# Two attention-and-spectral layers on one core: a second pair of row-sum accumulators, the row-sum matmul moved behind a product with V, the last group's output sums and the weights' maxima redistributed

## The chip, the cores and the metric

The kernel runs on 1 core of one Trainium2 chip. The metric is device time in microseconds (us) of one execution; a kernel's time is the median of its runs. TensorE (PE in the profile; its weight loads are PEld) does the matrix products, VectorE (DVE) elementwise work and reductions, ScalarE (ACT) the exponentials, copies and casts, GpSimd (POOL) small elementwise work, and SyncE (SP) issues nearly all transfers. Matmul results lie in PSUM, everything else on the chip in SBUF.

## The reference

x is 2048 rows of 1024. Two layers follow each other, with the same weights, and each is an attention block and a spectral block:

```python
def _A_ref(x, wqkv, wo):
    qkv = (x @ wqkv).reshape(B, S, 3, H, Dh).transpose(2, 0, 3, 1, 4)     # H = 32, Dh = 32
    q, k, v = qkv[0], qkv[1], qkv[2]
    scores = einsum("bhqd,bhkd->bhqk", q, k) * (Dh ** -0.5)
    o = einsum("bhqk,bhkd->bhqd", softmax(scores), v)
    return o.transpose(0, 2, 1, 3).reshape(B, S, D) @ wo

def _B_ref(x, w_r, w_i):
    X = rfft2(x, axes=(-2, -1)) * (w_r + 1j * w_i)
    return irfft2(X, s=(S, D), axes=(-2, -1))

for _ in range(2):
    x = x + _A_ref(_layernorm(x), A_wqkv, A_wo)
    x = x + _B_ref(_layernorm(x), B_w_r, B_w_i)
```

All values are float32. The kernel splits many operands into a high and a low float16 part and adds three products. That needs the inputs to lie in a range, so while it runs it gathers maxima of the weights and of a few statistics ("flags"); at the end `combine_flags` makes one number of them, by which a general version of the whole would run instead. With these inputs it does not run.

## The kernel before

**Layers.** `build` calls `attention` (L270) and `spectral` (L750) for layer 0 and layer 1. Layer 0 alone gathers the weights' maxima.

**Attention: start.** Rows are normalised, split and transposed by transfers, and the first values, keys and queries are made.

**Attention: the loop (L625 to L676).** The 32 heads are 8 groups `g` of 4. For each group there are 4 chunks `c` of 512 queries, and for each chunk 16 tiles `kt` of 128 keys. One step (g, c, kt) is:

- `S`: 12 matmuls (L558), 32 rows of the array each, give the scores of 4 heads in two PSUM tiles of 128x1024. The pool `psS` has 3 such tiles. ScalarE makes two exponentials `p` of 128x1024 from them (L562); the pool for `p` has 8 tiles, so four steps.
- `PV`: 4 products of `p` with V (L568), each in 32 columns of the array, added up over kt in PSUM (`psO`, one tile). They run two steps at a time, at even kt, for the two steps before.
- `add`: VectorE adds the two halves of `p` to the accumulators `acc` (L581; at kt = 1 it starts them from two tiles, L579).

When the last key tile of a chunk has been added, `fin` follows, at kt = 1 of the next chunk, after that step's scores: 4 matmuls with a matrix of ones (L587) turn `acc` into row sums in a third `psS` tile, VectorE transposes it, takes reciprocals, transposes back and scales the output (L588 to L594). At kt = 5 `out` splits the output into two float16 parts (L600, L601) and stores it, or keeps it in SBUF in the last group.

Two steps make a slot, kt even and kt odd. At the end of each slot TensorE gets other work as a fill, from generators that yield after each matmul or two: keys, queries and values of the next groups (L340, L384), and, in the last two groups, the product with the output weights. There a row tile t (128 rows, of chunk t // 4) is done in two parts. `wo_part` does the first 7 of 8 head groups: per half of 512 columns 21 matmuls (L443) and one VectorE eviction onto the residual (L466). `wo_rest` does the eighth group when its output is there: 6 matmuls into a `psS` tile, one 128x1024 eviction (L475), two statistics (L477), a store (L478), their aggregation (L498). Tiles 0 to 11 are done so inside the loop, tiles 2 and 3 partly in group 6. In group 7 a slot has either 21 matmuls of a part or one `wo_rest`; the first eleven slots have parts, and later the two alternate.

**Attention: the tail (L677 to L733).** The last chunk's row sums and output, then row tiles 12 to 15 (`first`, `last`, `whole`), and the other tiles are normalised and folded into the layout of the spectral block (L513, L146, L147).

**Spectral.** A first stage of 32 steps transposes (L791), multiplies (L800) and splits with ScalarE and VectorE (L804, L805). Beside it `absmax` loads the output weights in 16 pieces through 3 buffers and takes their maxima (L784, L785). Then a loop over 32 units (`fb`, `fc`, `binv`, `cinv`): products with constants (L862), copies (L855), products (L894), four VectorE products with the spectral weights (L901 to L904), GpSimd sums, a cast and its low half (L909, L910), and products back (L862, L931). `loadw` loads the weights two units ahead (L834) and takes their maxima (L837, L838). A last stage goes back to rows (L965, L977).

**Order.** TensorE's and ScalarE's order in the attention loop is the program's. Elsewhere, and on VectorE, GpSimd and SP everywhere, a planner fixes the order when the kernel is built, by its own estimate of when each instruction's inputs are there; at run time each engine takes its instructions strictly in that order. So an instruction of the spectral block can stand on VectorE inside the attention's tail.

Of the kernel before, what the change touches and what calls it, by code (L numbers as in the profile page):

```python
# [6 lines left out]
F32 = mybir.dt.float32  # L7
# [181 lines left out]
class AttnPools:  # L189


    def __init__(self, tc):
# [12 lines left out]
        self.acc = [a[:, i] for i in (14, 15)]  # L205
# [21 lines left out]
class Weights:  # L227
# [5 lines left out]
    def prep(self, ph):  # L233
# [36 lines left out]
def attention(nc, tc, layer, ap, xin, yd, wts, wo, cst, dram, flags):  # L270
# [184 lines left out]
    def wo_part(c, t, dst):  # L455

        x = xres(c, t)
        for n in range(2):
            p = bank()
            m = wo_mm(p, c, t, n, range(7))  # L460
            for _ in range(20):
# [4 lines left out]
            nc.vector.scalar_tensor_tensor(dst[:, sl], p, 1.0 / (SO * SW), x[:, sl], op0=ALU.mult, op1=ALU.add)  # L466
            yield
# [15 lines left out]
    def wo_parts():  # L483
        load_o(0)
        load_o(1)
        for t in [2, 3, 0, 1] + list(range(4, 12)):
# [7 lines left out]
    mvs = sm.tile([128, 24], F32, name="mvs")  # L494
# [55 lines left out]
    P, O, acc = {}, {}, ap.acc  # L550
# [24 lines left out]
    def add(g, c, kt):  # L575
        for hf in range(2):
            p = P[g, c, kt, hf]
            if kt == 1:
                nc.vector.scalar_tensor_tensor(acc[hf], P[g, c, 0, hf], 1e-34, p, op0=ALU.add, op1=ALU.add)  # L579
            elif kt:  # L580
                nc.vector.tensor_add(acc[hf], acc[hf], p)  # L581

    def fin(g, c):
        zt = on.tile([128, 16, 32], F32, name="zt")
        z = psS.tile([128, 2, 512], F32, name="s")[:, 0]
        for h in range(4):
            nc.tensor.matmul(z[32 * h:32 * h + 32], cst["ones"], acc[h // 2][:, h % 2], start=True, stop=True)  # L587
# [19 lines left out]
    pend, done, late = [], [], []  # L607
    fill, lwo, wof = filler(), load_wo(), wo_parts()
    left, parts, rests = 16, 20, list(range(12))
# [15 lines left out]
    with tc.manual_schedule(engines={mybir.EngineType.PE, mybir.EngineType.Activation}):  # L625
        for g in range(NG):
# [610 lines left out]
```

## Time and profile before

| | |
|---|---|
| median of 3 runs | 3885.8 us (3885.0 to 3886.59) |
| the profiled execution's own time | 3887.92 us |
| its span, first to last instruction | 3886.0 us |
| mean granted clock of TensorE | 0.988 |
| exponentials (L562) | 2048 x 1112 ns |
| additions to the accumulators (L581) | 1792 x 1218 ns |
| matmuls of a row sum (L587) | 512 records x 593 ns (median), 8 per row sum |
| running maxima, removed by the change: L261, L785, L838 | 48, 16 and 32 on VectorE |

How to read it: in an answer in order of time, each row has the start, the length, the engine, the line and operation, what is written and read, the count of instructions merged into the row, and in brackets the idle time of the engine just before, with what ended it. Lengths of instructions that follow each other overlap a little, so the time that one really takes is the distance between starts. In a view of one line the three figures are the shortest, the median and the longest in ns.

### The profile page before, as it was taken

Reading aid. Unit: us, or ns where it says so; the run is one execution under the profiler, and the core shown is the slowest. Engines: PE = TensorE matmul, PEld = TensorE weight load, DVE = VectorE, ACT = ScalarE, POOL = GpSimd, SP = SyncE. Lnnn points to the kernel's source line nnn. Section 1 sums busy time; section 2 is a strip of 40 time slices with the busy share of each in tenths; the row PEclk is TensorE's granted clock in tenths of the full one; section 3 lists DMA queues with packets and bytes.
Section 4 is the critical chain, followed back from the end, with each engine's and each line's share of the span. In section 5 each row is a group of like instructions: output and inputs, shape, how many; then the busy total and the mean of one; then the engine's idle time right before and its main releaser. Section 6 shows DMA issues by size and latency. Waiting matters only on the chain.

```text
span 3886.0 us, 79635 instructions
## 1 busy us (share of the span) xinstructions
PE 3738.1 (96%) x32951; PEld 1644.2 (42%) x32951; DVE 3181.9 (82%) x3967; ACT 2901.1 (75%) x3567; POOL 304.1 (8%) x386
## 2 busy tenths in 40 slices
PE   6999999999999999989989999999999999999998
PEld 4322433343234233368854334333433432333788
DVE  6689899989998987966675998989899889788544
ACT  4578887888788865657855888888888888666686
POOL 1000000000000000014320000000000000000143
PEclk9999999999999999999999999999999999999999
DMA  8000000000000221134270000000000002111333
GB/s 204 15 12 23 12 12 17 18 12 18 12 26 7 73 70 64 62 142 140 62 179 12 15 23 12 12 18 18 12 20 12 23 12 90 53 69 66 147 99 105
DMA packets 165575, 194.08 MB, mean 50 GB/s; under 512 B 74961, under 2 KB 120657, under 8 KB 164177
## 3 DMA queue, kind: packets, MB, share of 16 engines
q1 hardware_dynamic: 164912, 188.82, 15.6%
q8 instruction: 260, 4.26, 0.5%
q14 instruction: 115, 0.93, 0.1%
q10 hardware_dynamic: 288, 0.07, 0.0%
HBM read 123.83 MB, written 48.23 MB: 44 GB/s over the span
## 4 chain that ended last, share of the span: by engine, by line
PE 73%; DVE 12%; issue 7%; ACT 3%; DMA 3%; POOL 1%; SPq 0%; DVEq 0%; ACTq 0%; POOLq 0%
PE o L568 20%; PE s L558 17%; PE x L340 12%; PE x L384 7%; PE x L443 6%; DVE R L581 3%; ACT p L562 2%; PE ps L862 2%; PE ps L800 2%; PE s L587 1%; PE ps L791 1%; DMA w<-in_w 1%; PE s L443 1%; PE o L384 1%; PE ps L977 1%
## 5 line engine op out<-in xcount | busy, mean ns | idle before, releaser
L562 ACT ACTIVATE p<-s,bias 128x1024 f32<-128x1024 f32 x2048 | 2169.7, 1112 | 575.4 <-PE s L558 564.5
L581 DVE TENSOR_TENSOR R<-R,p 128x1024 f32<-128x1024 f32 x1792 | 2089.0, 1218 | 139.4 <-ACT p L562 136.3
L568 PE MATMUL o<-p,R 128*32 128x512 f32 x8192 | 985.5, 599 | 0.0
L340 PE MATMUL x<-big,wqk 128*128 128x512 f16 x2880 | 684.2, 383 | 17.0 <-DVE Q L168 6.3
L558 PEld LDWEIGHTS <-R 32*128 32x128 f16 x12288 | 233.0, 92 | 769.3 <-issue 654.3
L340 PEld LDWEIGHTS <-wqk 128*128 128x128 f16 x3072 | 277.3, 98 | 452.9 <-issue 159.1
L558 PE MATMUL s<-Q,R 32*128 32x512 f16 x6144 | 433.0, 378 | 12.0 <-ACT p L562 10.7
L558 PE MATMUL s<-R 32*128 32x512 f16 x6144 | 432.3, 379 | 8.2 <-ACT p L562 6.7
L568 PEld LDWEIGHTS o<-p,R 128*32 128x32 f32 x8192 | 213.8, 109 | 524.6 <-issue 524.0
L384 PEld LDWEIGHTS <-big 128*128 128x128 f16 x3072 | 296.5, 100 | 155.5 <-issue 73.9
L384 PE MATMUL x<-wv,big 128*128 128x256 f16 x2688 | 324.1, 277 | 34.5 <-DMA big<-hl 34.5
L579 DVE SCALAR_TENSOR_TENSOR R<-p 128x1024 f32<-128x1024 f32 x128 | 153.9, 1203 | 196.1 <-ACT p L562 195.7
L443 PE MATMUL x<-big 128*128 128x512 f16 x1050 | 237.4, 380 | 0.0
L365 POOL PARTITION_ALL_REDUCE mall<-mqk x16 | 40.7, 2542 | 2333.8 <-DVE mqk L359 2322.5
L443 PEld LDWEIGHTS <-big 128*128 128x128 f16 x1344 | 126.2, 98 | 178.0 <-issue 34.6
L910 DVE TENSOR_TENSOR H<-G,H 128x512 f16<-128x512 f32 (+1 forms) x68 | 46.5, 683 | 105.4 <-ACT H L909 105.3
L862 PE MATMUL ps<-cbi,H 128*128 128x256 f16 (+1 forms) x792 | 99.2, 273 | 6.0 <-ACT H L909 3.7
L855 ACT COPY U<-ps 64x256 f32<-64x256 f32 (+1 forms) x272 | 97.2, 357 | 8.4 <-PE ps L862 3.3
L855 ACT COPY B<-ps 64x256 f32<-64x256 f32 (+1 forms) x272 | 97.1, 357 | 6.7 <-PE ps L862 2.4
L862 PE MATMUL ps<-cb,big 128*128 128x256 f16 x780 | 96.3, 273 | 0.0
L805 DVE TENSOR_TENSOR big<-ps,big 128x512 f16<-128x512 f32 x64 | 44.5, 695 | 58.5 <-ACT big L804 58.5
L167 ACT ACTIVATE R<-x 128x512 f16<-128x512 f32 x88 | 52.7, 598 | 50.5 <-PE x L340 50.4
(429 smaller groups left out, 2992.5 us busy)
## 6 DMA issues: line engine op xcount, KB each, us to landing
wst<-in_wp SPq DMA_DIRECT2D x96, 256.0 KB, 3.0
R<-y SPq DMA_DIRECT2D x32, 512.0 KB, 5.4
w<-in_w SPq DMA_DIRECT2D x60, 256.0 KB, 2.7
od<-ohl SPq DMA_DIRECT2D x56, 256.0 KB, 2.4
big<-od SPq DMA_DIRECT2D x16, 896.0 KB, 6.7
y<-R SPq DMA_DIRECT2D x20, 512.0 KB, 2.7
R<-in_x SPq DMA_DIRECT2D x16, 512.0 KB, 5.8
wst<-in_wo SPq DMA_DIRECT2D x32, 256.0 KB, 3.0
```

The lines of the kernel that those rows point to most:

```text
L167: nc.scalar.activation(hi, src, AF.Copy, scale=scale)
L340: nc.tensor.matmul(ps, a, b, start=d == 0 and i == 0, stop=d == 7 and i == 2)
L384: nc.tensor.matmul(ps[:, j], l, r, start=d == 0 and i == 0, stop=d == 7 and i == 2)
L443: nc.tensor.matmul(p, a, b, start=start and d == ds[0] and i == 0, stop=stop and d == ds[-1] and i == 2)
L558: nc.tensor.matmul(s[h // 2][:, h % 2], K[g][r, a, kt * 128:kt * 128 + 128], Q[g][r, b, c * 512:c * 512 + 512], start=i == 0, stop=i == 2)
L562: nc.scalar.activation(p, s[hf], AF.Exp, bias=bias[g], scale=SCALE / (SQ * SQ))
L568: nc.tensor.matmul(O[g, c][32 * h:32 * h + 32], V[g][:, kt, 32 * h:32 * h + 32], P[g, c, kt, h // 2][:, h % 2], start=kt == 0, stop=kt == ...
L579: nc.vector.scalar_tensor_tensor(acc[hf], P[g, c, 0, hf], 1e-34, p, op0=ALU.add, op1=ALU.add)
L581: nc.vector.tensor_add(acc[hf], acc[hf], p)
L800: nc.tensor.matmul(pa[:, j], tt[:, j], mm[:, g], start=True, stop=True)
L855: nc.scalar.copy(ov[64 * r:64 * r + 64, a0:a0 + m, x], tl[64 * x:64 * x + 64, :m, r])
L862: nc.tensor.matmul(out, l, r, start=k == 0, stop=k == len(mm_) - 1)
```

## The change

1. **Accumulators.** There are now two pairs, `acc0` where the pair was and `acc1` in a new pool of its own; chunk c uses pair c % 2. The reserve for transfer descriptors in SBUF is given as 4096 bytes, and the new pair lies in the space.
2. **Row sums.** `add` of the last key tile now only notes the chunk in `full`; `fin` runs at kt = 2 of the next chunk, right behind that step's two products with V. The fin of the last chunk stays in the tail.
3. **The last group.** `share` gives for each of the 32 slots how many matmuls of `wo_part` it does (21 in ten slots, 7 in six, 11 and 10 in twelve, 12 in four), and `rests` in which slots a `wo_rest` follows them. Tile 11 is done in the last four slots with all 8 head groups at once, with its statistics and store, and has no `wo_rest`.
4. **Maxima.** Each reduction of a piece of the weights writes a column of its own in a table; the running maxima (L261, L785, L838) go, and `combine_flags` reduces the two tables at the end. The reductions of the output weights are held in program order: each stands on VectorE behind the instruction that the program has before it, which is a subtraction of the first spectral stage (L805).

```diff
-        self.acc = [a[:, i] for i in (14, 15)]
+        self.acc0 = [a[:, i] for i in (14, 15)]
...
+        self.accp = small("at_acc", 1)
...
-                wm = ap.sm.tile([128, 1], F32, name="wm")
-                nc.vector.tensor_reduce(wm, st[i], axis=AX.XY, op=ALU.max, apply_absolute_value=True)
-                nc.vector.tensor_max(self.flag, self.flag, wm)
+                nc.vector.tensor_reduce(self.flag.pop(), st[i], axis=AX.XY, op=ALU.max, apply_absolute_value=True)
...
-    def wo_part(c, t, dst):
+    def wo_part(c, t, dst, nd):
 
         x = xres(c, t)
+        st = sm.tile([128, 2, 6], F32, name="st")
         for n in range(2):
             p = bank()
-            m = wo_mm(p, c, t, n, range(7))
-            for _ in range(20):
+            m = wo_mm(p, c, t, n, range(nd))
+            for _ in range(3 * nd - 1):
                 next(m)
                 yield
             run(m)
             sl = slice(n * 512, n * 512 + 512)
             nc.vector.scalar_tensor_tensor(dst[:, sl], p, 1.0 / (SO * SW), x[:, sl], op0=ALU.mult, op1=ALU.add)
+            if nd == 8:
+                nc.vector.bn_stats(st[:, n], dst[:, sl])
+                if n:
+                    r0 = c * 512 + t * 128
+                    nc.sync.dma_start(yd[r0:r0 + 128, :], dst)
+                    nc.vector.bn_aggr(mvs[:, 8 * c + 2 * t:8 * c + 2 * t + 2], st)
             yield
...
-            yield from wo_part(t // 4, t % 4, wo_dst[t])
+            yield from wo_part(t // 4, t % 4, wo_dst[t], 8 if t == 11 else 7)
...
-    P, O, acc = {}, {}, ap.acc
+    P, O = {}, {}
+    acc1 = ap.accp.tile([128, 2, 2, 512], F32, name="acc")
+    acc = [ap.acc0, [acc1[:, i] for i in range(2)]]
...
-            nc.tensor.matmul(z[32 * h:32 * h + 32], cst["ones"], acc[h // 2][:, h % 2], start=True, stop=True)
+            nc.tensor.matmul(z[32 * h:32 * h + 32], cst["ones"], acc[c % 2][h // 2][:, h % 2], start=True, stop=True)
...
-    left, parts, rests = 16, 20, list(range(12))
+    left, rests = 16, {}
+    share = [21] * 10 + [7] * 6 + [11, 10] * 6 + [12] * 4
+    for t, n in zip(range(11), (11, 12, 14, 15, 20, 22, 24, 26, 28, 29, 30)):
+        rests[n] = t
...
                     late = pend
                     pend = []
+                    if kt == 2 and full:
+                        done = [full.pop()]
+                        fin(*done[0])
                 for w in late[:1]:
                     add(*w)
                     if w[2] == NKT - 1:
-                        fin(*w[:2])
-                        done = [w[:2]]
+                        full = [w[:2]]
...
                 elif g == NG - 1:
-                    t = rests[0] if rests else 16
-                    if (t // 4 < c - 1 or t // 4 == c - 1 and kt >= 7) and (kt % 4 == 3 or not parts):
-                        wo_rest(rests.pop(0))
-                    elif parts:
-                        parts -= 1
-                        for _ in range(21):
-                            next(wof)
+                    for _ in range(share[u // 2]):
+                        next(wof)
+                    if u // 2 in rests:
+                        wo_rest(rests[u // 2])
...
-            m = p3.tile([128, 1], F32, name="wom")
-            nc.vector.tensor_reduce(m, wos.pop(0), axis=AX.X, op=ALU.max, apply_absolute_value=True)
-            nc.vector.tensor_max(flags["w"], flags["w"], m)
+            tc.keep_in_program_order(nc.vector.tensor_reduce(flags["wcol"].pop(), wos.pop(0), axis=AX.X, op=ALU.max, apply_absolute_value=True))
...
-            m = p2.tile([128, 1], F32, name="wbm")
-            nc.vector.tensor_reduce(m, wt, axis=AX.X, op=ALU.max, apply_absolute_value=True)
-            nc.vector.tensor_max(flags["wb"], flags["wb"], m)
+            nc.vector.tensor_reduce(flags["wb"][:, i:i + 1], wt, axis=AX.X, op=ALU.max, apply_absolute_value=True)
...
+    fw, fb = (pool.tile([128, 1], F32, name=n) for n in ("fwm", "fwbm"))
+    nc.vector.reduce_max(fw, flags["w"], axis=AX.X)
+    nc.vector.reduce_max(fb, flags["wb"], axis=AX.X)
...
-    nc = _bacc.Bacc("TRN2", target_bir_lowering=False, num_devices=1)
+    nc = _bacc.Bacc("TRN2", target_bir_lowering=False, num_devices=1, dynamic_dma_scratch_size=4096)
```

More of the change, by code (lines that the diff above doesn't have):

```diff
@@ L453, in xres @@
         return x
-    def wo_part(c, t, dst):
+    mvs = sm.tile([128, 24], F32, name="mvs")
+    def wo_part(c, t, dst, nd):
         x = xres(c, t)
+        st = sm.tile([128, 2, 6], F32, name="st")
         for n in range(2):
             p = bank()
-            m = wo_mm(p, c, t, n, range(7))
-            for _ in range(20):
+            m = wo_mm(p, c, t, n, range(nd))
+            for _ in range(3 * nd - 1):
                 next(m)
@@ L485, in wo_parts @@
         load_o(1)
-        for t in [2, 3, 0, 1] + list(range(4, 12)):
+        for t in (2, 3, 0, 1, 4, 5, 6, 7, 8, 9, 10, 11):
             if t == 8:
@@ L605, in out @@
             olast[c] = t
-    pend, done, late = [], [], []
+    pend, done, late, full = [], [], [], []
     fill, lwo, wof = filler(), load_wo(), wo_parts()
-    left, parts, rests = 16, 20, list(range(12))
+    left, rests = 16, {}
+    share = [21] * 10 + [7] * 6 + [11, 10] * 6 + [12] * 4
+    for t, n in zip(range(11), (11, 12, 14, 15, 20, 22, 24, 26, 28, 29, 30)):
+        rests[n] = t
     def slots(f, sums, n, steps):
@@ L674, in attention @@
         run(wof)
-        for t in rests:
-            wo_rest(t)
     with tc.manual_schedule(engines={mybir.EngineType.PE}):
@@ L1173, in build @@
             "mv": cp.tile([128, 32, 2], F32, name="fmv"),
-            "w": cp.tile([128, 1], F32, name="fw"),
-            "wb": cp.tile([128, 1], F32, name="fwb"),
+            "w": cp.tile([128, 64], F32, name="fw"),
+            "wb": cp.tile([128, 32], F32, name="fwb"),
             "r": cp.tile([128, 16], F32, name="fr"),
@@ L1178, in build @@
         }
-        nc.vector.memset(flags["w"], 0.0)
-        nc.vector.memset(flags["wb"], 0.0)
+        flags["wcol"] = [flags["w"][:, i:i + 1] for i in range(64)]
         nc.vector.memset(flags["r"], 0.0)
@@ L1187, in build @@
             nc.sync.dma_start(ap.x[:, t], x[t * 128:(t + 1) * 128, :])
-        wts = [Weights(nc, ap, a["wp"], None if layer else flags["w"]) for layer in range(2)]
+        wts = [Weights(nc, ap, a["wp"], None if layer else flags["wcol"]) for layer in range(2)]
         for layer in range(2):
```

15 lines of the change are left out of this document (8 added, 7 removed).

## The prediction

> **What bounds the kernel now.** I read the page first, then the windows by stage, then the instructions in order of time.
>
> ```profile
> span 3886.0 us, 79635 instructions
> PE 3738.1 (96%) x32951; PEld 1644.2 (42%) x32951; DVE 3181.9 (82%) x3967; ACT 2901.1 (75%) x3567; POOL 304.1 (8%) x386
> PE 73%; DVE 12%; issue 7%; ACT 3%; DMA 3%; POOL 1%; SPq 0%; DVEq 0%; ACTq 0%; POOLq 0%
> ```
>
> TensorE is the bound of the whole, but 4% of the span is not its own. The windows (columns: stretch, its length, busy time of PE, PEld, DVE, ACT and POOL, granted clock, DMA) show where: the last head group of layer 0, then the attention's tail up to the first transpose of the spectral part in layer 0 and layer 1, then the spectral unit loop in layer 0 and layer 1.
>
> ```profile
> 1410.00:1640.00 230.00, 225.15 (x1798) 74.66 (x1787) 186.02 (x203) 138.80 (x136) 0.00 (x0) 1.00 0.17 62
> ...
> 1647.25:1705.26 58.01, 42.88 (x205) 18.76 (x201) 49.28 (x105) 20.14 (x21) 11.62 (x33) 0.90 0.48 161
> 3573.45:3621.30 47.85, 42.72 (x205) 18.77 (x201) 39.43 (x74) 20.03 (x21) 11.64 (x33) 0.98 0.27 95
> ...
> 1755.11:1918.43 163.32, 153.10 (x1303) 135.95 (x1300) 104.45 (x256) 132.45 (x340) 70.49 (x102) 1.00 0.32 104
> 3670.60:3822.39 151.79, 147.59 (x1303) 134.26 (x1300) 73.97 (x190) 130.51 (x340) 70.65 (x102) 1.00 0.36 113
> ```
>
> In the attention loop TensorE has almost nothing to regain by waiting less: only what its own blocks cost, and small bubbles. The two layers do the same matmuls (205 and 205, 1303 and 1303), yet layer 0 is 10.2 us longer in the tail and 11.5 us longer in the unit loop. What layer 0 has more is VectorE work, 9.9 and 30.5 us of it: the weights' maxima. So the change touches three places that set the time.
>
> **Part 1: the row-sum behind a product with V.** TensorE in order of time around one row-sum of the last group (scores L558, products with V L568, row-sum L587, output sums L443):
>
> ```profile
> 1480.13 1.92 PE L568 MATMUL o<-p,R 128*32 128x512 f32 x16
> 1481.99 0.83 PE L558 MATMUL s<-Q,R 32*128 32x512 f16 x12
> ...
> 1482.74 1.06 PE L587 MATMUL s<-R,ones 128*32 128x512 f32 x8
> ...
> 1483.74 4.71 PE L443 MATMUL x<-big 128*128 128x512 f16 x21
> ...
> 1488.38 0.83 PE L558 MATMUL s<-Q,R 32*128 32x512 f16 x12
> ```
>
> No row-sum here waits: scores start to row-sum start is 0.75, the usual length of a scores block. The row-sum takes 1.00 (1482.74 to 1483.74). It has the shape of one product with V, of which two in one block take 1.86 (1480.13 to 1481.99). If a block costs a fixed s and m per step, 2m+s = 1.86 and m+s = 1.00, so m = 0.86 and s = 0.14. Behind the products, in their shape, the row-sum costs m alone and saves s.
>
> ```profile
> L587 PE MATMUL s<-R,ones x512: 589/593/617, 175.9 to 3583.1; 128*32 128x512 f32 x171
> ```
>
> 512 records by 8 are 64 row-sums; one per layer lies in the tail and stays, so 62 x 0.14 = 8.7 us. Before shows no row-sum behind a product, so the ends are 0 (the next block pays the switch all the same) and 8.7; I take 8.7, because the two steps inside a product block are that very case. The Trainium skill, "TensorEngine Tiling (Array Packing)", section "Key Properties", says that changing the tiling mode, not just the tile, drains the array; by that rule the whole of s goes, and by a switch that the scores pay anyway nothing would; no run here shows it yet.
>
> The second accumulator pair takes away VectorE's wait at each chunk for the row-sum to have read the first. VectorE isn't the bound there, so 0 us; it is cover for part 2. The price is a hidden one: the row-sum's PSUM tile now starts later, and rival A is about that. The smaller descriptor reserve costs nothing while all transfers are of hardware queues; the tiles that move in SBUF may shift a first load by a microsecond or two, either way.
>
> **Part 2: the last group dealt anew.** Before, a slot (two key tiles) has either 21 output matmuls or a closing of 6 (L472 to L478). TensorE and VectorE around a closing:
>
> ```profile
> 1507.01 0.82 PE L558 MATMUL s<-Q,R 32*128 32x512 f16 x12
> 1507.77 1.47 PE L443 MATMUL s<-big,ohl 128*128 128x512 f16 x6
> ...
> 1509.02 1.23 DVE L581 TENSOR_TENSOR R<-R,p 128x1024 f32<-128x1024 f32 x1 [0.25 <-ACT p L562]
> 1509.17 0.39 PE L558 MATMUL s<-Q,R 32*128 32x512 f16 x2
> 1510.05 0.82 PE L558 MATMUL s<-Q,R 32*128 32x512 f16 x10 [0.48 <-ACT p L562]
> 1510.16 1.22 DVE L475 SCALAR_TENSOR_TENSOR R<-s,R 128x1024 f32<-128x1024 f32 x1
> ...
> 1511.30 1.22 DVE L581 TENSOR_TENSOR R<-R,p 128x1024 f32<-128x1024 f32 x1
> 1512.43 1.28 DVE L477 BATCH_NORM_STATS2 st<-R 128x6 f32<-128x512 f32 x2
> 1512.65 0.83 PE L558 MATMUL s<-Q,R 32*128 32x512 f16 x12
> 1513.63 1.21 DVE L581 TENSOR_TENSOR R<-R,p 128x1024 f32<-128x1024 f32 x1
> 1514.75 0.20 DVE L498 BATCH_NORM_AGGREGATE mvs<-st 128x2 f32<-128x12 f32 x1
> ...
> 3566.75 0.82 PE L558 MATMUL s<-Q,R 32*128 32x512 f16 x10 [0.48 <-ACT p L562]
> ```
>
> After a short closing the next scores wait 0.48 us: the closing holds the third PSUM tile and only 1.4 us have passed for two exponentials.
>
> ```profile
> PE s L558 <- ACT p L562: 17.4, 29, 1.8
> ```
>
> 22 of these 29 waits, 11 per layer, from 1510.05 to 3566.75, are of this kind: 22 x 0.48 = 10.6 us. After the change every closing has 7 to 12 matmuls ahead of it, so the exponentials are done. That is the gain's end: -10.6.
>
> What takes its place is VectorE. A closing costs it 1.14 (1510.16 to 1511.30) + 1.20 (1512.43 to 1513.63) + about 0.15 = 2.5 us, four additions cost 4 x 1.13 = 4.53, and a half tile's eviction is as long as one L477, 0.60. TensorE has 0.75 + 1.86 + 0.75 = 3.36 per slot without fill; 21 matmuls take 4.64 (1483.74 to 1488.38), 6 take 1.40 (1507.77 to 1509.17), so a matmul is 0.216 and a block 0.10. In slots 11, 12, 14 and 15 (7 matmuls and a closing) TensorE needs 3.36 + 0.10 + 13 x 0.216 = 6.27 and VectorE 4.53 + 2.5 + 0.2 = 7.23. Four times 0.96, with slot 10 (+0.36, an output's low half) and 13 (-0.24), make VectorE 4.0 us late by the end of that chunk. In slots 16 to 27 a slot without closing is 5.73 against 4.83, so it recovers; in 28 to 30 both need about 7.3. The lateness is free until the closing's PSUM tile is missed: here L475 ends at 1511.38 and the scores that need the tile start at 1512.65, so 1.3 of 4.0 are free and 2.7 us per layer are lost. Net -10.6 + 5.4 = -5.2. The bounds: -10.6 (buffers hide all of it) and about 0 (all lateness shows, with some 1.2 more per layer in the later closings).
>
> **Part 3: the weights' maxima.** In layer 0 the 16 reductions of the output weights (L784) run inside the tail, ahead of what the tail waits for:
>
> ```profile
> 1691.11 0.81 PE L443 MATMUL x<-big,ohl 128*128 128x512 f16 x3
> ...
> 1697.69 1.27 DVE L784 TENSOR_REDUCE wom<-wo 128x1 f32<-128x512 f32 x2
> 1698.88 0.68 DVE L706 SCALAR_TENSOR_TENSOR xres<-x,xres 128x512 f32<-128x512 f32 x1
> ```
>
> The last sum is there by 1691.9 and its eviction starts at 1698.9, behind reductions. Held in program order they come behind the low-half subtractions of the first spectral stage, so the tail becomes that of layer 1: -10.2 (58.01 to 47.85). That stage has room:
>
> ```profile
> 3632.02 0.69 DVE L805 TENSOR_TENSOR big<-ps,big 128x512 f16<-128x512 f32 x1 [0.78 <-ACT big L804]
> ```
>
> VectorE idles 0.78 us per step and gets one reduction of 0.6 us every second step. If that cover were gone, 16 x 0.6 = 9.6 us would come back; bounds -10.2 and 0, I take -10.2. The pinning adds a wait on SP: from the fourth on, each load of output weights waits for a reduction. Queued behind are the reload of the rows and the first two spectral weights:
>
> ```profile
> 1755.35 0.81 SPq L834 DMA_DIRECT2D w<-in_w  x2
> ```
>
> They go out only as the first stage ends (the unit loop starts at 1755.11), and the last reduction falls just ahead of that, so I count 0; a microsecond late would be a microsecond on the path.
>
> In the unit loop the maximum over the running one (L838) goes, its reduction stays:
>
> ```profile
> 1800.03 0.69 DVE L910 TENSOR_TENSOR H<-G,H 128x512 f16<-128x512 f32 x1 [1.35 <-ACT H L909]
> ...
> 1802.09 0.15 DVE L838 TENSOR_TENSOR fwb<-fwb,wbm 128x1 f32<-128x1 f32 x1
> ...
> 1805.10 0.69 DVE L910 TENSOR_TENSOR H<-G,H 128x512 f16<-128x512 f32 x1 [2.05 <-ACT H L909]
> ...
> 1807.16 0.58 DVE L838 TENSOR_TENSOR fwb<-fwb,wbm 128x1 f32<-128x1 f32 x1
> 1807.66 0.41 DVE L903 TENSOR_TENSOR G<-ps,w 128x256 f32<-128x256 f32 x1
> ```
> ```profile
> L838 DVE TENSOR_TENSOR fwb<-fwb,wbm x32: 147/571/580, 1761.1 to 1908.7; 128x1 f32<-128x1 f32 x32
> ```
>
> It sits between products that the next steps wait for and takes 0.50 there (1807.16 to 1807.66) in the long form, at least 16 of 32 by the median; the short form costs under 0.1. TensorE is held by this chain in layer 0 (163.32 against 151.79), so the bounds are 0 and -11.5; I take 16 x (0.50 - 0.07) = -7. The other maxima gone, 48 in the weights' preparation, lie under a busy TensorE except at the start: -0.3 with the two new reductions at the end. The Trainium skill, "VectorE: DVE Perf Modes", section "The DRAIN you can't avoid", has each operation wait until the pipe of the one before is empty; by its full 0.57 the 32 would come to 18 us, more than the 11.5 by which the layers differ, and the row above, where the next starts 0.50 behind, speaks for less.
>
> **Sum.** -8.7 - 5.2 - 10.2 - 7 - 0.3 = -31.4, against the profiled execution's span of 3886.0 (its own time was 3887.92). The span is 0.2 from the median 3885.8, so the median should come to 3854.
>
> **Rivals.** A, slower: the row-sum's tile is read late. From the row-sum's end TensorE needs one scores block, a fill and then the third PSUM tile. In a narrow slot that is 2.59 us:
>
> ```profile
> 323.95 0.83 PE L558 MATMUL s<-Q,R 32*128 32x512 f16 x12
> ...
> 326.54 0.83 PE L558 MATMUL s<-Q,R 32*128 32x512 f16 x12
> ```
>
> Before, the same tile had a product block more, 1.86. If VectorE's fixed order puts four additions (4.5) ahead of the transpose (0.7), the scores wait 2.6 us, in wider slots less, say 1.7 on average: 62 x 1.7 = 105, and 3960. It decides from 31.4 / 62 = 0.5 us per row-sum. For it: VectorE is over 90% busy there and its order is planned, not written. Against: the additions of the next step aren't ready until its exponentials are, so at most two lie ahead, and 2.3 + 0.7 = 3.0 costs 0.4 in narrow slots only. Chance 0.08.
>
> B: VectorE becomes the last group's bound, part 2 gives nothing and part 1 half: -22, 3864. Chance 0.15. C: the maxima don't leave the path: the reductions cost the spectral stage what the tail gains, or the unit loop stays as it is because the reduction of 0.6 alone holds it: 10 to 17 us less gain, 3868. For it: those reductions stay in both. Chance 0.17. D: the change doesn't do what it says: the scores pay the switch that the row-sum saves, the late VectorE eats part 2 and C's two failures come together: 3880 to 3886, chance 0.05.
>
> The forecast keeps 0.55. Faster by over 0.2% (7.8 us, about what a measurement tells from no change) is forecast, B, C and a fifth of D: 0.88; within 0.2%: 0.04; slower: 0.08. The range goes from 3844 (parts 2 and the loop at their full ends) to 3871 (C); A is left out.
>
> **What would show it.** Right: L587 starts behind L568 and the next L558 comes 0.86 later; no 0.48 bubbles in the last group; layer 0's tail near 48 us, its unit loop near 156. Wrong: scores waiting on the row-sum's transpose at a chunk's third step (A), VectorE without a gap and scores waiting in the last group's second chunk (B), L784 still ahead of L706, or a first spectral stage over 50 us (C).

## The result and the profile after

| | before | changed |
|---|---|---|
| median, runs of both on the same chip | 3885.4 us (3882.65 to 3886.59, 4 runs) | 3862.59 us (3856.95 to 3865.57, 4 runs) |
| profiled execution: its own time, its span | 3887.92, 3886.0 us | 3861.45, 3858.3 us |
| mean granted clock of TensorE | 0.988 | 0.991 |

The ratio is 0.9936, 95% interval 0.9924 to 0.9948: faster by 0.52 to 0.76%. The medians differ by 22.8 us, the two profiled spans by 27.7. The prediction had 31.4 in spans and a median of 3854, so the kernel came out 8.6 us above the forecast and inside its range (3844 to 3871). The head of the changed kernel's page, and its chain of waits (share of the span by engine):

```profile
span 3858.3 us, 79444 instructions
PE 3712.9 (96%) x32951; PEld 1644.9 (43%) x32951; DVE 3175.5 (82%) x3869; ACT 2896.5 (75%) x3567; POOL 308.5 (8%) x386
PE 39%; DVE 7%; issue 5%; ACT 2%; POOL 2%; DMA 1%; SPq 0%; DVEq 0%; POOLq 0%; ACTq 0%
```

TensorE is still busy for 96%, with 25 us less busy time for the same 32951 matmuls. The chain can't be set beside the one of before (its shares add up to 56% of the span here, to 99% before), so the comparison goes by stage. Windows of the changed kernel in this order: the last group of layer 0; the tail and the unit loop of layer 0; then a middle group of layer 1 (columns as in the prediction):

```profile
1411.73:1638.50 226.77, 223.17 (x1822) 75.07 (x1821) 193.26 (x211) 139.44 (x136) 0.00 (x0) 1.00 0.20 69
1638.50:1686.29 47.79, 42.72 (x205) 18.77 (x201) 35.75 (x68) 19.99 (x21) 11.59 (x33) 1.00 0.32 109
1735.16:1897.34 162.18, 152.41 (x1303) 136.24 (x1301) 94.77 (x231) 132.03 (x340) 70.24 (x102) 0.99 0.35 112
2416.15:2596.03 179.88, 178.43 (x1611) 54.59 (x1611) 164.63 (x175) 148.35 (x155) 2.28 (x4) 1.00 0.05 16
```

The same group before:

```profile
2439.01:2617.85 178.84, 178.56 (x1612) 54.12 (x1612) 163.56 (x175) 148.60 (x155) 2.29 (x4) 1.00 0.05 16
```

All stages, from the start of one's first matmul to the start of the next one's:

| stage | before | changed | difference | predicted |
|---|---|---|---|---|
| groups 0 to 6, layer 0 | 1289.08 | 1287.70 | -1.4 | -3.8 |
| groups 0 to 6, layer 1 | 1265.21 | 1268.16 | +3.0 | -3.8 |
| last group, both layers | 2 x 232.95 | 2 x 226.77 | -12.4 | -6.3 |
| tail, both layers | 58.01 + 47.85 | 47.79 + 47.79 | -10.3 | -10.2 |
| unit loop, layer 0 | 163.32 | 162.18 | -1.1 | -7 |
| the rest (start, both first spectral stages, last stage of layer 0, start and unit loop of layer 1, end) | | | -5.5 | -0.3 |

The predicted 8.7 of the row-sums is dealt to the groups by their number here, 27 per layer in groups 0 to 6 and 4 in the last. The total came out near the forecast because misses of both signs nearly cancel: groups 0 to 6 became longer instead of shorter and the unit loop hardly moved, while the last group gained twice its share and the rest 5 us more than counted.

**The row-sum.** TensorE in order of time in the changed kernel, at a chunk's third step in layer 1 (scores L566, products with V L576, row-sum L596):

```profile
2422.11 1.92 PE L576 MATMUL o<-p,R 128*32 128x512 f32 x16
2423.85 1.04 PE L596 MATMUL s<-acc,ones 128*32 128x512 f32 x8
2424.83 0.83 PE L566 MATMUL s<-R 32*128 32x512 f16 x12
```

The saving is there. A product block with a row-sum behind it takes 1.74 (2422.11 to 2423.85) where one without takes 1.86 as before, and the row-sum 0.98: 2.72 together, where before it was 1.86 + 1.00 = 2.86. That is the 0.14 of the prediction, a little of it on either side of the seam. The group of which this is part is 1.04 us longer all the same (178.84 to 179.88). TensorE's waits in a group of the same kind (group 4 of layer 1), before and then changed:

```profile
PE s L558 <- DVE mqk L359: 0.2, 1, 0.2
```
```profile
PE x L339 <- DVE Q L168: 0.7, 1, 0.7
PE s L566 <- DVE mqk L358: 0.3, 1, 0.3
PE x L339 <- DVE R L168: 0.2, 1, 0.2
PE s L356 <- DVE sq L343: 0.2, 1, 0.2
```

1.2 us of new waits, all for VectorE. L168 is an eviction of new queries or keys: until it is done, the next fill has no PSUM bank. Why it is later shows in VectorE's own order at the start of a chunk, before:

```profile
2443.63 1.23 DVE L579 SCALAR_TENSOR_TENSOR R<-p 128x1024 f32<-128x1024 f32 x1 [3.74 <-ACT p L562]
2444.78 0.71 DVE L588 STREAM_TRANSPOSE zt<-s 128x512 f32<-128x512 f32 x1
2445.41 1.18 DVE L579 SCALAR_TENSOR_TENSOR R<-p 128x1024 f32<-128x1024 f32 x1
...
2457.98 0.68 DVE L168 SCALAR_TENSOR_TENSOR R<-x,R 128x512 f16<-128x512 f32 x1
```

and in the changed kernel:

```profile
2420.77 2.36 DVE L588 SCALAR_TENSOR_TENSOR R<-p 128x1024 f32<-128x1024 f32 x2 [3.74 <-ACT p L570]
2423.36 2.36 DVE L590 TENSOR_TENSOR R<-R,p 128x1024 f32<-128x1024 f32 x2 [0.23 <-ACT p L570]
2425.64 0.71 DVE L597 STREAM_TRANSPOSE zt<-s 128x512 f32<-128x512 f32 x1
...
2435.53 0.68 DVE L168 SCALAR_TENSOR_TENSOR R<-x,R 128x512 f16<-128x512 f32 x1
```

VectorE waits 3.74 us at the start of a chunk in both, and both times it is for the exponentials, not for a row-sum to have read the accumulators: the wait ends 4.62 after the group's first scores (2439.01 and 2416.15) with one pair and with two. Before, the row-sum's transpose stands right behind the first addition. Changed, the row-sum isn't there yet: VectorE makes two additions, waits 0.23 for exponentials, makes two more and only then has the row-sum's work, some 2.5 us (2425.64 to 2428.11, where the next additions start). The amount of work is the same, and in both kernels there is no gap before the eviction in which the 0.23 could be made up. Counted from the group's first scores the eviction starts at 18.97 before and 19.38 after: 0.41 late, and TensorE, which has just become quicker, waits.

**The last group.** TensorE's waits in it, layer 0, before and changed:

```profile
PE s L558 <- ACT p L562: 5.3, 11, 0.5
```
```profile
PE s L566 <- DVE R L483: 2.8, 3, 1.4
PE x L442 <- DVE R L468: 0.6, 1, 0.6
PE s L566 <- DVE wv L483: 0.2, 1, 0.2
```

The eleven bubbles are gone, and what came instead is VectorE's lateness: 3.0 for the closings' evictions (L483; the sum had 2.7) and 0.6 for a half tile's. The waits fall by only 1.7, and yet the group is 6.18 shorter. The rest lies in what a bubble breaks. In the rows of before that the prediction shows, the scores start at 1509.17, stop after 2 of 12 matmuls and go on at 1510.05. The next row there is

```profile
1510.80 1.92 PE L568 MATMUL o<-p,R 128*32 128x512 f32 x16
```

so the block took 1.63 where an undisturbed one takes 0.75 to 0.76. A bubble of 0.48 idle cost 0.87. No run takes back this part alone, but e6 below, without the moved row-sum and without the second pair, keeps the shorter group (226.37).

**The tail.** VectorE in the changed kernel, layer 0, at the last sum's eviction (L715, formerly L706):

```profile
1681.25 0.69 DVE L715 SCALAR_TENSOR_TENSOR xres<-x,xres 128x512 f32<-128x512 f32 x1 [2.13 <-PE x L442]
```

Now VectorE waits for TensorE there, where before TensorE's finished sum lay for 7 us until VectorE came.

**The unit loop.** SyncE's queue where the first stage of layer 0 ends (1735.16), changed:

```profile
1733.88 0.38 SPq L789 DMA_DIRECT2D wo<-in_wo  x1
...
1738.95 0.81 SPq L841 DMA_DIRECT2D w<-in_w  x2
```

Before, the first spectral weights were asked for 0.24 after the unit loop's start (1755.35 against 1755.11). Now it is 3.79 after it. What they wait for, from the view of SyncE's waits:

```profile
SPq L841 <- DVE fw L792: 3.6, 1, 3.6
```

L792 is the pinned reduction of the output weights. The last of the 16 loads of them goes out at 1733.88, behind the reduction that frees its buffer, so the last reduction starts only at 1738.12 and lasts 0.69; the spectral weights go out right behind it. TensorE pays twice, in the changed kernel:

```profile
1747.46 0.39 PE L867 MATMUL ps<-cbi,H 128*128 128x256 f16 x2 [4.21 <-ACT H L914]
...
1748.27 2.34 PE L867 MATMUL ps<-cbi,H 128*128 128x256 f16 x10
```
```profile
1747.46:1752.46 5.00, 5.00 (x31) 3.80 (x32) 3.19 (x9) 1.77 (x5) 2.14 (x3) 0.66 0.97 341
```

It idles 4.21 us, and then the granted clock of the next 5 us is 0.66: ten matmuls take 2.34. The same place before, where the wait was 1.56 and the clock stayed at 1.00:

```profile
1765.09 0.39 PE L862 MATMUL ps<-cbi,H 128*128 128x256 f16 x2 [1.56 <-ACT H L909]
...
1765.81 1.27 PE L862 MATMUL ps<-cbi,H 128*128 128x256 f16 x10
```
```profile
1765.09:1770.09 5.00, 4.42 (x38) 3.60 (x39) 4.24 (x11) 4.30 (x12) 2.14 (x3) 1.00 0.99 351
```

2.65 of idle time and (1 - 0.66) x 5 = 1.7 of clock make some 4.4 us. The Trainium skill, "TensorE: Matmul & The Clock Gate", section "Part 1: The HAM clock gate (the "warmup" mystery)", says that about 3.4 us without work halve the clock until TensorE has been busy as long again. This trace agrees only in part: 4.21 did it here, and after a wait of 2.63 in layer 0 of the changed kernel the next 12 matmuls took 2.75, as elsewhere, but after one of 2.34, two groups later, they took 4.27:

```profile
613.14 2.75 PE L339 MATMUL x<-big,wqk 128*128 128x512 f16 x12 [2.63 <-DVE Q L168]
...
978.90 4.27 PE L339 MATMUL x<-big,wqk 128*128 128x512 f16 x12 [2.34 <-DVE Q L168]
```

The granted clock over the 4 us from there is 0.63 (978.90 to 982.90). So here a wait well under 3.4 us can cost clock too, and its length alone doesn't decide.

### The profile page after: what moved, and what is told of

It reads as the page before. It is cut to its first block, busy times and chain, and to the rows that moved or that the text cites. A ratio compares the mean times of both kernels' runs of the same rounds, so it can differ in the third digit from the quotient of the medians.

```text
span 3858.3 us, 79444 instructions
## 1 busy us (share of the span) xinstructions
PE 3712.9 (96%) x32951; PEld 1644.9 (43%) x32951; DVE 3175.5 (82%) x3869; ACT 2896.5 (75%) x3567; POOL 308.5 (8%) x386
## 4 chain that ended last, share of the span: by engine, by line
PE 39%; DVE 7%; issue 5%; ACT 2%; POOL 2%; DMA 1%; SPq 0%; DVEq 0%; POOLq 0%; ACTq 0%
PE o L576 9%; PE s L566 8%; PE x L339 6%; PE x L383 4%; PE x L442 3%; PE ps L867 2%; PE ps L807 2%; DVE acc L590 1%; PE s L442 1%; PE ps L798 1%; PE ps L982 1%; DVE R L590 1%; DMA w<-in_w 1%; PE ps L936 1%; ACT p L570 1%
## 5 line engine op out<-in xcount | busy, mean ns | idle before, releaser
L590 DVE TENSOR_TENSOR R<-R,p 128x1024 f32<-128x1024 f32 x896 | 1042.0, 1220 | 63.2 <-ACT p L570 62.3
L590 DVE TENSOR_TENSOR acc<-acc,p 128x1024 f32<-128x1024 f32 x896 | 1043.7, 1219 | 49.0 <-ACT p L570 47.4
L576 PE MATMUL o<-p,R 128*32 128x512 f32 x8192 | 985.8, 599 | 0.0
L566 PEld LDWEIGHTS <-R 32*128 32x128 f16 x12288 | 230.9, 92 | 763.6 <-issue 647.9
L566 PE MATMUL s<-R 32*128 32x512 f16 x6144 | 432.2, 378 | 11.7 <-ACT p L570 8.1
L576 PEld LDWEIGHTS o<-p,R 128*32 128x32 f32 x8192 | 213.8, 109 | 524.8 <-issue 524.8
L566 PE MATMUL s<-Q,R 32*128 32x512 f16 x6144 | 425.2, 378 | 7.1 <-DVE R L483 5.5
L588 DVE SCALAR_TENSOR_TENSOR R<-p 128x1024 f32<-128x1024 f32 x64 | 75.6, 1222 | 111.4 <-ACT p L570 111.4
L915 DVE TENSOR_TENSOR H<-G,H 128x512 f16<-128x512 f32 (+1 forms) x68 | 45.8, 674 | 115.3 <-ACT H L914 115.2
L588 DVE SCALAR_TENSOR_TENSOR acc<-p 128x1024 f32<-128x1024 f32 x64 | 75.7, 1222 | 70.7 <-ACT p L570 70.7
```

Source lines behind the costliest of these rows:

```text
L566: nc.tensor.matmul(s[h // 2][:, h % 2], K[g][r, a, kt * 128:kt * 128 + 128], Q[g][r, b, c * 512:c * 512 + 512], start=i == 0, stop=i == 2)
L576: nc.tensor.matmul(O[g, c][32 * h:32 * h + 32], V[g][:, kt, 32 * h:32 * h + 32], P[g, c, kt, h // 2][:, h % 2], start=kt == 0, stop=kt == ...
L588: nc.vector.scalar_tensor_tensor(t, P[g, c, 0, hf], 1e-34, p, op0=ALU.add, op1=ALU.add)
L590: nc.vector.tensor_add(t, t, p)
L915: nc.vector.tensor_sub(lo, gs, hi)
```

## The experiments

In e1 to e8 each kernel was executed once, with a profile. The kernel before, beside them on the same chip, took 3890.26 (e1 to e4) and 3885.81 (e5 to e8). e9 and e10 were timed in rounds. One caution for all: layer 0's groups carry dips of the clock that differ from execution to execution. Two executions of one and the same kernel (e1 and e10) have 188.08 at clock 0.98 and 190.45 at 0.96 for its first group. The middle groups of layer 1 run at 1.00 and agree to 0.01.

**e1: the row-sum back at the next chunk's second step, all else as changed.**

```diff
-                    if kt == 2 and full:
-                        done = [full.pop()]
-                        fin(*done[0])
...
-                        full = [w[:2]]
+                        fin(*w[:2])
+                        done = [w[:2]]
```

> The changed kernel with the row-sum matmul back at the second step of the next chunk, after its scores; both accumulator pairs, the redealt last group and the maxima stay. Theory 1 (the row-sum behind the products saves 0.15 us each, but the waits that it used to cover show instead: the norm matmuls and the evictions on VectorE): groups 0 to 6 of both layers together within 4 us of the changed kernel, the norm waits back to 0.7 us per odd group in layer 1, the last group 0.3 to 0.6 us longer, span 3856 to 3861. Rival (the saving is there and something else in the loop, such as the new place of the tiles in SBUF, takes it): groups 0 to 6 about 8 us longer, span 3866.

It took 3850.46, less than either theory gave, and the last group, expected 0.3 to 0.6 longer, takes 226.67 (226.77 changed). Layer 1's groups are back at the lengths of before, 180.68 and 178.84, and so are the waits; group 4 of layer 1 in e1:

```profile
PE s L566 <- DVE mqk L358: 0.2, 1, 0.2
```

All waits of TensorE in groups 0 to 6, the rows of that view added up by group:

| | before | changed | e1 | e10 (e1 again) | e2 |
|---|---|---|---|---|---|
| layer 0 | 25.2 | 30.9 | 23.6 | 23.2 | 30.9 |
| layer 1 | 11.0 | 18.7 | 11.9 | 12.4 | 20.1 |

The moved row-sum adds 49.6 - 35.5 = 14.1 us of waits in these groups and saves 54 x 0.14 = 7.6 us of work. It is a loss of some 6 us. In lengths, where a wait that breaks a block costs more than its idle time, layer 1's groups 0 to 7 are 3.75 longer than e1's; layer 0's are 6.8 longer than in e1 and 3.4 longer than in e10.

Layer 0 shows something else besides. In each of its groups 1 to 5 TensorE has one long wait for VectorE: 1.90 to 2.24 us before, 2.34 to 3.20 changed, 1.64 to 1.84 in e1 and e10. Behind three of the five waits before, and three of the five changed, the granted clock was 0.57 to 0.63 over the next 4 us; behind all ten in e1 and e10 it was 1.00, and behind one of five in e9 (1.78) it was 0.57. These five groups take 918.0 before, 915.9 changed, 911.1 in e1 and 910.4 in e10, and 910.5 in e6, which has parts 3 and 4 alone. The same groups of layer 1 take 899.7 in before, e1, e6 and e10. So something in the change shortens layer 0's groups by some 7 us, and the late row-sum hides most of it. What only layer 0 has there, and the change removes, are the running maxima of the weights' preparation (L261). No run takes them back alone, and of before there is one trace, so this cause is argued and not shown.

**e2: the norms later.** In odd groups the longest new wait is that of the norm matmuls (L356) for their squares: 1.36 in group 1 of layer 1, where it was 0.73 before. Counted from the group's first scores, TensorE comes to them 0.28 earlier (68.14 against 68.42) and VectorE to the eviction ahead of the squares 0.34 later (68.82 against 68.48). Here the norms come behind that slot's fill.

```diff
-                while left_norms:
-                    norms()
+                held = len(left_norms)
...
+                for _ in range(held):
+                    norms()
```

> The changed kernel with the norm matmuls behind the fill of their slot instead of ahead of it. Theory 1 (the row-sum's saving is lost mainly because the norms now wait for VectorE's squares): the waits of the norms, 13.5 us over both layers, shrink to under 3 us, odd groups of layer 1 become 180.1 or less (before 180.68, changed 180.75), even ones stay near 179.6, span 3846 to 3851. Rival (VectorE is late as a whole there, and the wait only moves to the scores that need the norm's PSUM tile): the groups stay within 0.3 us, span 3856 to 3860.

3859.6. An odd group takes 180.41 instead of 180.75, between what the two theories gave, and the wait moves on; group 1 of layer 1 in e2:

```profile
PE x L383 <- DVE R L168: 1.4, 1, 1.4
```

So it is not one badly placed instruction: VectorE as a whole is behind, and TensorE meets that wherever it next needs it.

**e3: the unit loop without its reductions.** This kernel leaves out the 32 maxima of the spectral weights and writes a constant in their place.

```diff
-        if flags is not None:
-            nc.vector.tensor_reduce(flags["wb"][:, i:i + 1], wt, axis=AX.X, op=ALU.max, apply_absolute_value=True)
...
+        nc.vector.memset(flags["wb"], 0.01)
```

> The changed kernel without the reductions of the spectral weights in the unit loop: their maxima are left out and stand in as a constant. Theory 2 (after the change it is the reduction of 0.6 us between the products that holds layer 0's unit loop; dropping the running maximum only took slack): unit loop of layer 0 from 162.2 to 152.9, as in layer 1, span 3849. Rival (layer 0's loop is longer for another reason, such as its weights' transfers or the granted clock): it stays over 159, span 3855 to 3858.

3853.49, and layer 0's unit loop takes 151.74, that of layer 1 (151.79 before). The reductions themselves hold the loop; the removed maxima over the running one were only a part of it.

**e4: the output weights' reductions not pinned.**

```diff
-            tc.keep_in_program_order(nc.vector.tensor_reduce(flags["wcol"].pop(), wos.pop(0), axis=AX.X, op=ALU.max, apply_absolute_value=True))
+            nc.vector.tensor_reduce(flags["wcol"].pop(), wos.pop(0), axis=AX.X, op=ALU.max, apply_absolute_value=True)
```

> The changed kernel with the reductions of the output weights left to the planner instead of held in program order. Theory 3 (what shortened the tail of layer 0 is their place, not the removed running maxima): the tail of layer 0 is back at 56 to 58 us (changed 47.8, before 58.0), span 3866 to 3869. Rival (the removed running maxima did it, 16 of them with their waits): tail under 52, span 3858 to 3862.

3867.22. Windows of e4, the tail and the unit loop of layer 0, and its queue and first wait there:

```profile
1641.38:1696.14 54.76, 42.72 (x205) 18.79 (x201) 45.06 (x87) 20.10 (x21) 11.51 (x33) 0.92 0.50 163
1745.80:1903.55 157.75, 151.20 (x1303) 135.56 (x1300) 92.89 (x225) 132.37 (x340) 70.14 (x102) 1.00 0.35 113
```
```profile
1746.03 0.81 SPq L841 DMA_DIRECT2D w<-in_w  x2
...
1755.75 0.39 PE L867 MATMUL ps<-cbi,H 128*128 128x256 f16 x2 [1.53 <-ACT H L914]
```

The tail lies between what the two theories gave. In it the removed running maxima are worth 3.25 (58.01 to 54.76), the place of the reductions 7.0 (54.76 to 47.79). But the weights are asked for 0.23 after the loop's start again, the wait is 1.53, and the loop takes 157.75: 4.43 less than in the changed kernel, which is the 4.4 worked out above from idle time and clock. So the pinning nets 2.5 of the 7.0.

**e5: one accumulator pair, the row-sum late.**

```diff
-        self.accp = small("at_acc", 1)
...
-    acc1 = ap.accp.tile([128, 2, 2, 512], F32, name="acc")
-    acc = [ap.acc0, [acc1[:, i] for i in range(2)]]
+    acc = [ap.acc0, ap.acc0]
```

> The changed kernel with one accumulator pair for all chunks, the row-sum still behind the products. Theory 4 (VectorE stands at each chunk's start for the first exponentials, not for the row-sum, so the second pair is only needed because the row-sum now comes later): with one pair the first additions must wait for the row-sum at the third step, some 4 us later than the exponentials; VectorE, which has no gap for the next 20 us, evicts later and TensorE waits: even groups of layer 1 over 182 us (changed 179.9), span over 3870. Rival (VectorE's buffers take up 4 us): groups within 0.5 us of the changed kernel, span 3854 to 3862.

4039.25, far above the 3870 that was expected at least. VectorE can't start a chunk before the row-sum (here L594) has read the last one's accumulators, and then has no gap until 2551.1. VectorE in order of time, TensorE's waits in the same group (group 2 of layer 1), and TensorE with the granted clock behind the first of them:

```profile
2531.64 1.22 DVE L586 SCALAR_TENSOR_TENSOR R<-p 128x1024 f32<-128x1024 f32 x1 [7.95 <-PE s L594]
```
```profile
PE x L338 <- DVE R L168: 5.4, 2, 3.6
PE x L338 <- DVE Q L168: 4.1, 1, 4.1
PE s L355 <- DVE sq L342: 2.9, 1, 2.9
```
```profile
2546.32 3.57 PE L338 MATMUL x<-big,wqk 128*128 128x512 f16 x8 [3.60 <-DVE R L168]
```
```profile
2546.00:2550.50 4.50, 4.18 (x16) 1.31 (x19) 4.50 (x6) 0.00 (x0) 0.00 (x0) 0.50 0.18 60
```

The second pair is needed for the late row-sum: without it the group takes 196.27. 12.4 of its extra time are waits, and behind a wait of 3.60 the clock was 0.50 (eight matmuls in 3.57, elsewhere 1.90).

**e6: one pair and the row-sum back**, the edits of e1 and e5 together; what is left of the change is the last group and the maxima.

> One accumulator pair and the row-sum back at the second step, the redealt last group and the maxima as in the changed kernel: parts 3 and 4 alone. Theory 4: the second pair brings nothing where the row-sum is early, so all groups of layer 1 are as in the run with the row-sum back (178.84 and 180.68, last group 226.7), span 3845 to 3850. Rival (the second pair frees VectorE at the chunk starts): groups longer by a microsecond or more, last group over 228.

3858.74, which I had expected lower, yet within what e1's kernel took in six executions (3846.44 to 3859.84). By the trace the groups are e1's: 178.83 and 180.68, waits 22.7 + 11.6 against 23.6 + 11.9. One stage differs: layer 0's last one takes 47.90 in e5 and e6, as before, and 45.8 in every kernel with the second pair. In it TensorE waits 1.6 us for VectorE's L988 before (L989 in e6), and 0.4 for the same line (L993) in the changed kernel.

**e7: e1, with the output weights' maxima done earlier**: two in each three steps, from the first step of the stage to step 23, not one every second step to its end.

```diff
-        if i % 2:
-            absmax(i // 2)
+        if i < 24 and i % 3 < 2:
+            absmax(i // 3 * 2 + i % 3)
```

> The row-sum back at the second step, and the 16 pieces of output weights taken in two of every three steps of the first spectral stage from its start, so that the last is done by step 23 of 32. Theory 5 (in the changed kernel the last pinned reductions hold the first spectral weights' load back by 3.7 us, and that hides what the removed running maxima gave the unit loop): first weight load of layer 0 within 0.4 us of the unit loop's start, unit loop 157 to 159 (changed 162.2), tail 47.8, span 3842 to 3845. Rival (the load is late for another reason): unit loop 162, span 3847.

3845.77; layer 0's unit loop takes 158.37, its first stage 48.85 and the tail stays at 47.79. The gain of the pinning is had without its price.

**e8: e7, with each unit's maximum taken a unit later**, held in program order behind the four products of the unit before.

```diff
-            nc.vector.tensor_reduce(flags["wb"][:, i:i + 1], wt, axis=AX.X, op=ALU.max, apply_absolute_value=True)
+            tc.keep_in_program_order(nc.vector.tensor_reduce(flags["wb"][:, i:i + 1], wt, axis=AX.X, op=ALU.max, apply_absolute_value=True))
...
+            if flags is not None and o == 0:
+                readyw(i + 1)
```

(`readyw` is the second half of `loadw`, from the reduction on.)

> As the run before it, and in the unit loop each unit's maximum is taken one unit later than its load, held behind the products of the unit before, where VectorE idles for 1.8 us. Theory 2 (the reduction between the products is what still holds layer 0's unit loop): unit loop of layer 0 152 to 154, span 3837 to 3840. Rival (the reduction only has to be somewhere, or the later sign products on GpSimd hold the next unit): 157 or more, span 3842 to 3848.

3836.02; the unit loop takes 149.90, less than either theory gave. VectorE in one of its steps, changed kernel and then e8 (four products, L906 to L909 and L915 to L918; the reduction, L843 and L852):

```profile
1785.24 0.42 DVE L907 TENSOR_TENSOR t__19449<-ps,w 128x256 f32<-128x256 f32 x1
1785.58 0.68 DVE L843 TENSOR_REDUCE fwb<-w 128x1 f32<-128x512 f32 x1
...
1788.90 0.69 DVE L915 TENSOR_TENSOR H<-G,H 128x512 f16<-128x512 f32 x1 [1.84 <-ACT H L914]
```
```profile
1784.70 0.41 DVE L918 TENSOR_TENSOR t__19572<-ps,w 128x256 f32<-128x256 f32 x1
1785.03 0.67 DVE L852 TENSOR_REDUCE fwb<-w 128x1 f32<-128x512 f32 x1
...
1786.99 0.69 DVE L926 TENSOR_TENSOR H<-G,H 128x512 f16<-128x512 f32 x1 [0.89 <-ACT H L925]
```

The reduction has not become shorter. Among the products it delays everything behind them, and VectorE then idles 1.84 for ScalarE's cast; behind the products it lies in that idle time, of which 0.9 is left.

**e9 and e10: e8's kernel and e1's, timed in rounds** beside the kernel before (3886.53, 8 runs).

> The kernel of e8 again (row-sum matmuls before the product with V, the weights' maxima spread over the steps of the first stage, each unit's maximum taken one unit later), timed in rounds. Theory 1 (what e8 showed is of the kernel: units at 149.9 us in both layers, groups of layer 1 at 178.84 and 180.68): the median is 3832 to 3840 us, a ratio of 0.986 to 0.989 to the kernel before. Theory 2 (e8 was a favourable single look, since layer 0's groups scatter by 2 us each from kernel to kernel): over 3842 us, with layer 0's groups 0 to 6 longer than in e8 by the difference.

> The kernel of e1 again (the changed kernel with the row-sum matmul at its old place, all else as changed), timed in rounds. Theory 1 (the later row-sum is a net loss, some 3.75 us in layer 1 by the two traces and about as much or more in layer 0): the median is 3847 to 3856 us, a ratio of 0.990 to 0.992, with no overlap of its interval with the changed kernel's 0.9924 to 0.9948. Theory 2 (the later row-sum is worth nothing either way, and e1's 3850 is scatter of layer 0): 3858 to 3866 us, a ratio of 0.993 to 0.995.

e9: 3836.28 (3836.14 to 3840.71, 4 runs), ratio 0.9873, interval 0.9857 to 0.9889. It is the best version found, 26 us below the changed kernel's median, with a unit loop of 148.73.

e10: 3854.53 (3846.44 to 3859.84, 5 runs), ratio 0.9920, interval 0.9906 to 0.9934. The median is 8.1 below the changed kernel's, about what the waits and lengths say, but the intervals overlap (the changed kernel's begins at 0.9924), which I had not expected. By whole times alone the row-sum's loss isn't settled; it rests on the waits and on layer 1's groups, which repeat (180.68 and 178.84 again).

## Why the prediction was right, and where it was wrong

**Part 1, the row-sum: the step that failed.** The 0.14 per row-sum was right to the hundredth. What failed is "VectorE isn't the bound there, so 0 us", and with it that the whole 8.7 was taken as gain. That in the loop TensorE has "almost nothing to regain by waiting less" holds for before, but it doesn't say that TensorE can't lose by waiting more. Over a whole group VectorE is busy for 164 of 179 us, but for long stretches of a chunk it has no gap at all, and most of its idle time lies at the chunk's start. The row-sum's work came later into such a stretch, VectorE lost 0.23 us to idling ahead of it, and the eviction behind came 0.41 late. Predicted -8.7; e1 against the changed kernel makes it about +6 by the waits. Nothing in part 1 set TensorE's saving against the moment at which VectorE delivers. Rival A had VectorE's order as the cause, but the wrong victim: the row-sum's own tile is never waited for, and the cost per row-sum is 0.1, not 1.7.

**The second pair.** I wrote that it takes away VectorE's wait for the row-sum to have read the first pair. Before has no such wait: its 3.74 ends at an exponential, with the row-sum just over (2442.38 to 2443.44), and with two pairs it is 3.74 as well. e6 shows the pair worth nothing to the groups with the early row-sum; e5 shows that the late one can't do without it.

**Part 2, the last group: right mechanism, one term mis-sized.** The bubbles went and VectorE's lateness came, at 2.7 predicted and 3.0 measured per layer, with 0.6 for a half tile's eviction that the sum lacked. The term "22 x 0.48" was too small: by the block's starts it is 0.87 each, 19.1 in all. With 1.1 for the eight row-sums, 19.1 + 1.1 - 2 x 3.6 = 13.0 stands near the measured 12.4. Rival B's condition came partly true (scores do wait for L483), without eating the gain.

**Part 3, the tail: right**, -10.22 for -10.2. e4 splits it into 3.25 for the removed running maxima and 7.0 for the new place.

**Part 3, the unit loop: the size near, the cover wrong.** With the weights' load in time the removed maxima are worth 5.6 (e4) or 5.0 (e7), where I took 7. They showed as 1.1, because of the line "the last reduction falls just ahead of that, so I count 0". It ended 3.65 behind (1738.81 against 1735.16), and the weights waited for that reduction itself. The price I gave, a microsecond for a microsecond, was too low: the weights went out 3.55 later than before, and that cost 2.65 of idle time and 1.7 of clock. Rival C's form of this (the reduction alone holds the loop) is true of what is left: the loop takes 151.74 without it (e3), and is no longer than that with it in a better place (149.90 and 148.73, e8 and e9).

**What the sum did not have.** Some 5 us in small stages: 1.2 at the start and 1.7 at the end, 2.1 in layer 0's last stage, 1.0 and 0.5 in the first spectral stages, with 1.1 back in layer 1's unit loop. The 2.1 go with the second pair's place in SBUF (e5 and e6 lack it); what in that place does it was not tried. Layer 1's unit loop took 150.22 to 151.79 in two executions of one kernel (e10, e1), so its 1.1 is of the size of the scatter. And for the 48 maxima of the weights' preparation the sum had -0.3, because they "lie under a busy TensorE". If the 7 us by which layer 0's groups 1 to 5 are shorter in e1, e6 and e10 are theirs, this term was some 7 too small.

So the forecast held by errors of both signs: against the sum, groups 0 to 6 and the unit loop fell short by 9 and 6 us, and part 2 and the small stages gave 6 and 5 more. In the groups themselves two errors meet: the moved row-sum's loss, and a gain in layer 0 that the sum didn't have. That the total came so near the forecast is luck.

## What to carry over

Before work is moved to a later place, look not at an engine's share over the stage but at where its idle time lies: VectorE idles at a chunk's start and has no gap for long afterwards, so 0.23 us that it lost there, with its work put in another order, made what stands behind 0.41 late, and TensorE's waits over 14 groups grew by 14.1. Read a bubble's cost from the starts of the blocks around it, not from the idle time. And where a reduction is pinned to a place, look for the loads that wait for it: here those of the next stage's weights waited 3.6 us for the last one.

## What the runs showed of the hardware

A wait can cost TensorE more than itself: behind 3.60 and 4.21 us of idle time the granted clock was 0.50 (over 4.5 us) and 0.66 (over 5 us). Shorter waits did so at times: 1.78 in e9, 1.90, 1.95 and 2.24 before and 2.34 in the changed kernel gave 0.57 to 0.63 over 4 us, while another of 1.95 and one of 2.02 before, and 2.63 and 2.92 in the changed kernel, left it at 1.00. A block of 12 scores that stops after 2 matmuls for 0.48 us took 0.87 longer. And eight row-sum matmuls behind products of the same shape took 0.14 less than behind scores, which take 32 rows of the array and not 32 columns.
